# Powers of the state-space basis made on GpSimd during attention, and a channel loop fed by few large transfers

## The chip, the cores and the metric

The kernel runs on one core of a Trainium2 chip. The metric is the device time of one execution in microseconds. Some executions fall into a second, slower state of the chip.

## The reference

The reference computes a layer and all its gradients. `x` has 2048 tokens of 576 channels. Three parts are mixed by a gate:

```python
g = sigmoid((x * gate_w).sum(-1, keepdims=True))
a = attention(x, wqkv, wo)                 # 32 heads of 18 dimensions, softmax
# state-space convolution, per channel d with N = 128 complex modes:
logdA = exp(log_dt)[:, None] * (A_re + 1j * A_im)
K[d, l] = Re sum_n C[d, n] * exp(logdA[d, n] * l) * exp(log_dt[d]) * B[d, n]
b = causal_convolution(x, K) + x * Dskip   # the reference does it by FFT
out = g * a + (1 - g) * b
# ... and the vjp of out for x, wqkv, wo, the state-space parameters and gate_w
```

The kernel cuts the sequence of each channel into 16 pieces of 128 tokens. It therefore needs, for each channel and mode, the powers `exp(logdA * l)` for `l` from 0 to 127. This table, 576 x 128 x 128 complex numbers, is the **basis** of the title.

## The kernel before

The program has these stages: projections and the products of dO (here "first stage"), attention forward and backward, the weight gradients, and a loop over 18 blocks of 32 channels for the state-space part, followed by a final stage. In attention and in the channel loop the instructions of four engines stand in program order. SyncE, which issues nearly all transfers, is not among them; its queue is laid out by the scheduler:

```python
ctx.enter_context(tc.manual_schedule(engines={PE, Activation, DVE, Pool}))
```

In attention, each finished group of four score gradients `ds` is transposed by a transfer, and each finished gradient tile goes by a transpose, a pack on GpSimd, and a store:

```python
nc.vector.tensor_tensor(U["ds"][i][:, j, :], ps, U["PT"][i][:, j, :], op=A.mult)     # ds: 4 buffers
...
    nc.sync.dma_start_transpose(out=U["dsT", p][:, i % 2, :, :], in_=U["ds"][i]...)   # every 4th product

def store_grad(gb, g, which, t0):
    gT = work.tile([P, TPQ, 4, HP], BF, tag="gT", name="gT")
    nc.sync.dma_start_transpose(out=gT..., in_=gb)
    dtk = work.tile([P, TPQ, 4, DH], BF, tag="dtk", name="dtk")
    nc.gpsimd.tensor_copy(dtk, gT[:, :, :, 0:DH])
    nc.sync.dma_start(dqkv_d[...], dtk...)
```

In the channel loop, every block makes its own basis and its own shifted copies of `x` (cuts are marked):

```python
def m_load(b):                                    # eight shifted copies of x, 7 of them in a chain
    nc.sync.dma_start(xs[:, 0, :, :], xsub[:, :, d0:d0 + CB])
    nc.sync.dma_start(gyp[:, 0:SUB, :], gsub[:, :, d0:d0 + CB])
    for dl in range(1, NSUB):
        nc.sync.dma_start(xs[dl:P, dl, :, :], xs[0:P - dl, 0, :, :])
def m_mask(b):                                    # VectorE clears what was shifted in
    ...
    for dl in range(1, NSUB):
        nc.vector.tensor_scalar(xs[:, dl, :, :], xs[:, dl, :, :], msk[:, dl:dl + 1], None, op0=A.mult)
def kk(b, h, q):                                  # phase on TensorE, rounded on ScalarE
    ph = B_["ph"][(h, q)] = phase(b, h, q, 0)
    nc.scalar.activation(B_["kk"][h][:, 4 * q:4 * q + 4, :], ph, ACT.Identity, bias=magc, scale=1.0)
def ff(b, h, q):                                  # reduced on VectorE
    nc.vector.scalar_tensor_tensor(v_, v_, MAGIC, B_["ph"].pop((h, q)), op0=A.subtract, op1=A.subtract)
def sn(b, h): ...                                 # two sines and a square on ScalarE
def prod(b, h):                                   # products on VectorE, then a transpose by DMA
    nc.vector.tensor_tensor(E_[:, :, 1, :], B_["kk"].pop(h), B_["ab"][h], op=A.mult)
    nc.vector.scalar_tensor_tensor(E_[:, :, 0, :], B_["uk"].pop(h), 1.0, B_["ab"].pop(h), ...)
    nc.sync.dma_start_transpose(out=En..., in_=E_...)
```

Of the kernel before, what the change touches and what calls it, by code (L numbers as in the profile page):

```python
# [17 lines left out]
P = 128  # L18


def build(tc, aps, dbg_aps=None, stages=("s1", "attn", "post", "s4", "final")):
# [39 lines left out]
    with ExitStack() as gctx:  # L61
# [36 lines left out]
        spl_d = dram.tile([2, 3, D, N], BF, name="spl_d")  # L98
# [3 lines left out]
        omg_d = dram.tile([S], F32, name="omg_d")  # L102
        Md_d = dram.tile([D, SUB, MW], F32, name="Md_d")
        Kp_d = dram.tile([D, 2 * P], BF, name="Kp_d")
# [7 lines left out]
        with ExitStack() as ctx:  # L112
# [63 lines left out]
            for c in range(DC):  # L176
                nc.sync.dma_start_transpose(out=woT[:, :, c * P:(c + 1) * P], in_=wo_pad[:, c, :])
            cnt = 0
# [35 lines left out]
            for t in range(NT):  # L214
                if t % TB == 0:
                    tb = t // TB
                    go_b = work.tile([P, TB, D], BF, tag="go_b", name="go_b")
                    nc.sync.dma_start(go_b, go_v[:, t:t + TB, :])
                    d_a = d_a2[tb % 2]
                    for q in range(TB):  # L220
                        nc.vector.tensor_scalar(d_a[:, q, 0:D], go_b[:, q, :], g_t[:, t + q:t + q + 1], None, op0=A.mult)
                    d_aT = work.tile([P, TB, DC, P], BF, tag="d_aT", name="d_aT")
                    nc.sync.dma_start_transpose(out=d_aT.rearrange("p t c q -> p (t c) q"), in_=d_a.rearrange("p t d -> p (t d)"))
                psd = psB.tile([P, 2, 512], F32, tag="dO", bufs=1, name="ps_dO")
# [11 lines left out]
            with nc.allow_non_contiguous_dma(reason="gate values regrouped by 16 tokens"):  # L236
                nc.sync.dma_start(omg_d.rearrange("(t p) -> p t", p=P), omg_t)
# [11 lines left out]
            zero_bf = s1.tile([P, P], BF, name="zero_bf")  # L249
            nc.vector.memset(zero_bf, 0.0)  # L250
            for c, (d0, dsz) in enumerate(dch):
                nc.sync.dma_start(Kp_d[d0:d0 + dsz, 0:P], zero_bf[0:dsz, :])
# [5 lines left out]
            ltc = s1.tile([P, DC], BF, name="ltc")  # L258
            nc.gpsimd.memset(ltc, 0.0)
            for c, (d0, dsz) in enumerate(dch):  # L260
                nc.sync.dma_start(ltc[0:dsz, c:c + 1], log_dt.rearrange("(d o) -> d o", o=1)[d0:d0 + dsz, :])
            dtc = s1.tile([P, DC], F32, name="dtc")
            nc.scalar.activation(dtc, ltc, ACT.Exp)
            dtci = s1.tile([P, DC], F32, name="dtci")
            nc.scalar.mul(dtci, dtc, INV2PI)
            prm = []
            for r_, src_ap in enumerate((A_re, A_im, B_re, B_im, C_re, C_im)):
# [9 lines left out]
                if r_ < 2:  # L277
                    spl = s1.tile([P, 3, DC, N], BF, tag="spl", name="spl")
                    for c, (d0, dsz) in enumerate(dch):
                        sc_ = work.tile([P, N], F32, tag="adn", name="adn")  # L280
                        nc.vector.tensor_scalar(sc_[0:dsz, :], blk_[0:dsz, c, :], (dtc, dtci)[r_][0:dsz, c:c + 1], None, op0=A.mult)
                        for q in range(3):
                            nc.vector.tensor_copy(spl[0:dsz, q, c, :], sc_[0:dsz, :])
                            if q < 2:
                                nc.vector.tensor_tensor(sc_[0:dsz, :], sc_[0:dsz, :], spl[0:dsz, q, c, :], op=A.subtract)
                            nc.sync.dma_start(spl_d[r_, q, d0:d0 + dsz, :], spl[0:dsz, q, c, :])
# [20 lines left out]
            def zpow(p, nm):  # L307
# [7 lines left out]
                sh = newt("gk")  # L315
                nc.scalar.activation(sh, v_, ACT.Sin, scale=0.5 * TWO_PI * SIN_SAFE)
                nc.scalar.activation(v_, v_, ACT.Sin, scale=TWO_PI * SIN_SAFE)
# [25 lines left out]
        if "attn" in stages:  # L343
# [5 lines left out]
            with ExitStack() as ctx:  # L349
# [78 lines left out]
                def grad_tile(tag):  # L428
                    return work.tile([P, KB], BF, tag="gb" + tag, name="gb")

                def store_grad(gb, g, which, t0):
                    c0 = which * D + g * 4 * DH
                    gT = work.tile([P, TPQ, 4, HP], BF, tag="gT", name="gT")
                    nc.sync.dma_start_transpose(out=gT.rearrange("p t a b -> p t (a b)"), in_=gb)
                    dtk = work.tile([P, TPQ, 4, DH], BF, tag="dtk", name="dtk")
                    nc.gpsimd.tensor_copy(dtk, gT[:, :, :, 0:DH])
                    nc.sync.dma_start(dqkv_d[:, t0:t0 + TPQ, c0:c0 + 4 * DH], dtk.rearrange("p t a b -> p t (a b)"))
# [30 lines left out]
                def dv_burst(g, b, kq, half):  # L468
# [8 lines left out]
                    def ev():  # L477
# [6 lines left out]
                        if b == NQ - 1 and half == 1:  # L484
                            o_ = DKV[("v", g, kq)] = grad_tile("v")
# [3 lines left out]
                def dq_burst(g, b, p):  # L489
# [8 lines left out]
                    def ev():  # L498
# [5 lines left out]
                        if p == NST // 4 - 1:  # L504
                            o_ = U["dqa"] = grad_tile("q")
# [3 lines left out]
                def dk_half(g, b, p, h, st):  # L509
# [13 lines left out]
                    def ev():  # L523
# [3 lines left out]
                        if b == NQ - 1:  # L527
                            if p % 2 == 0:
                                DKV[("kb", g, kq)] = grad_tile("k")
                            o_ = DKV[("kb", g, kq)]  # L530
# [4 lines left out]
                    return ev  # L535

# [7 lines left out]
                for g0, nm, g, m in sorted(lds):  # L544
                    if g0 < 0:
                        load_piece(nm, g, m)
                    else:
                        at(("pre", g0), lambda nm=nm, g=g, m=m: load_piece(nm, g, m))
                NTOT = NU * NST
                for G in range(NTOT + OFF + 16):  # L550
# [113 lines left out]
                assert not todo, todo.keys()  # L664
# [102 lines left out]
        if "s4" in stages:  # L767
            CB = 32
            XB = 2 * CB
            GS = 16  # L770
            NBLK = D // CB
# [5 lines left out]
            dDs_d = dram.tile([1, D], F32, name="dDs_d")  # L777
# [3 lines left out]
            with ExitStack() as ctx:  # L781
# [3 lines left out]
                ident_f4 = pc.tile([P, P], F32, name="ident_f4")  # L785
                nc.vector.tensor_copy(ident_f4, ident_bf)
# [6 lines left out]
                magc = pc.tile([P, 1], F32, name="magc")  # L793
                nc.vector.memset(magc, MAGIC)
                lrow_i = pc.tile([64, P], mybir.dt.int32, name="lrow_i")
                nc.gpsimd.iota(lrow_i, pattern=[[1, P]], base=0, channel_multiplier=0)
                lrow = pc.tile([64, P], BF, name="lrow")
                nc.vector.tensor_copy(lrow, lrow_i)
                omp = pc.tile([P, SUB], F32, name="omp")
                nc.sync.dma_start(omp, omg_d.rearrange("(p t) -> p t", t=SUB))  # L800
                sidx_i = pc.tile([P, 1], mybir.dt.int32, name="sidx_i")
                nc.vector.tensor_scalar(sidx_i, pidx_i, NSUB - 1, None, op0=A.bitwise_and)
                scol = pc.tile([P, 1], F32, name="scol")
                nc.vector.tensor_copy(scol, sidx_i)
                msk = pc.tile([P, NSUB], F32, name="msk")
                for dl in range(NSUB):
                    nc.vector.tensor_scalar(msk[:, dl:dl + 1], scol, float(dl) - 0.5, None, op0=A.is_gt)
# [6 lines left out]
                xs = pc.tile([P, NSUB, SUB, CB], BF, name="xs")  # L814
                nc.vector.memset(xs[0:NSUB], 0.0)
                gyp = pc.tile([P, 2 * SUB, CB], BF, name="gyp")
                nc.vector.memset(gyp[:, SUB:2 * SUB, :], 0.0)
# [8 lines left out]
                xsub = x2.rearrange("(p t) d -> p t d", t=SUB)  # L826
                gsub = go2.rearrange("(p t) d -> p t d", t=SUB)
# [7 lines left out]
                def load_rx(xb):  # L835
# [3 lines left out]
                    gob = pw.tile([P, NB, XB], BF, tag="gob", name="gob")  # L839
                    nc.sync.dma_start(gob, go_v[:, :, d0:d0 + XB])  # L840
                    RXs[xb] = (RX, gob)

                def prep_rx(xb):
                    RX, gob = RXs[xb]
                    nc.vector.tensor_tensor(RX[:, CV0:CV0 + NB, :], gob[:, ::-1, :],
                                            omg_t[:, ::-1].unsqueeze(2).to_broadcast([P, NB, XB]), op=A.mult)
                    nc.vector.tensor_scalar(RX[:, CU1:CU1 + NS, :], RX[:, CU0:CU0 + NS, :], l1col, None, op0=A.mult)
                    nc.vector.tensor_scalar(RX[:, CV1:CV1 + NS, :], RX[:, CV0:CV0 + NS, :], l0col, None, op0=A.mult)

                def m_load(b):  # L850
                    d0 = b * CB
                    nc.sync.dma_start(xs[:, 0, :, :], xsub[:, :, d0:d0 + CB])
                    nc.sync.dma_start(gyp[:, 0:SUB, :], gsub[:, :, d0:d0 + CB])
                    for dl in range(1, NSUB):
                        nc.sync.dma_start(xs[dl:P, dl, :, :], xs[0:P - dl, 0, :, :])

                def m_mask(b):
                    nc.vector.tensor_tensor(gyp[:, 0:SUB, :], gyp[:, 0:SUB, :], omp.unsqueeze(2).to_broadcast([P, SUB, CB]), op=A.mult)
                    for dl in range(1, NSUB):
# [525 lines left out]
```

## Time and profile before

The time was 3787.35 us, the median of three runs (3780.48 to 3792.01). Cut by first and last instructions of each stage, the profiled execution of 3788.0 us splits so:

| stage | us |
|---|---|
| first stage, to the first exponential of attention | 256.0 |
| attention, to the last store of a gradient tile | 2140.3 |
| weight gradients | 227.2 |
| ramp, to the first scan of the channel loop | 95.2 |
| channel loop, first to last scan (17 blocks of 52.6) | 893.6 |
| last block and final stage | 175.7 |

The prediction below shows the slices, the table of busy time, the loop's groups and a list of waits, whose columns are who waited for whom, the total in us, how often, and the longest. Two more views of the kernel before stand behind the prediction. The first is the waits of the engines within attention; the columns are who waited for whom, the total in us, how often, and the longest:

```profile
ACT PT L646 <- PE ps_P L30: 41.6, 43, 4.3
...
DVE ds L655 <- DMA dsT<-ds: 7.5, 7, 2.3
```

ScalarE, the bound of attention, hardly waits, and VectorE practically never waits for a transpose to free a `ds` buffer. The second is the same list for the SyncE queue, in the same stretch:

```profile
SPq L661 <- DVE ds L655: 1072.9, 410, 6.5
...
SPq L437 <- POOL dtk L436: 54.6, 38, 3.8
```

SyncE spends half of attention waiting for the next `ds`, which means that it has nothing else to do and that the transposes leave at once. The second line is the one to remember: the gradient stores wait in this queue for GpSimd's pack, 54.6 us in all. GpSimd is idle then. Its packs in turn wait for the transposed tile (91 times, 931.2 us), so what holds such a store is the chain of transpose and pack ahead of it.

### The profile page before, as it was taken

What the parts mean: (1) busy time and instruction counts of PE and PEld (TensorE: products, weight loads), DVE (VectorE), ACT (ScalarE), POOL (GpSimd) and SP (SyncE); (2) the same over time, 40 slices, a digit from 0 to 9 for tenths busy, and PEclk for the clock granted to TensorE, in tenths of its full rate; (3) what the DMA queues carried; (4) which work ended last, traced back from release to release, by engine and by line L of the source; (5) the groups of instructions that cost most, each with busy time, mean ns of one, the idle gap of its engine ahead of it and who ended that gap; (6) DMA issues with size and microseconds to landing.
All of it is one profiled execution on the core that took longest, in us unless ns stands there. A gap on an engine that the chain in (4) does not pass through costs nothing. (4 is left out here: it accounts for less than half of the span.)

```text
span 3788.0 us, 67550 instructions
## 1 busy us (share of the span) xinstructions
PE 2907.0 (77%) x25832; PEld 1159.2 (31%) x25832; DVE 2891.6 (76%) x5099; ACT 2769.8 (73%) x5125; POOL 106.0 (3%) x210
## 2 busy tenths in 40 slices
PE   7969999999999999999999999487355444544421
PEld 2322323323323323333233232244133333333310
DVE  4616888878888888888888888253488888888867
ACT  4539999999999999999999997110466666666610
POOL 0000000000000000000000000100000000000000
PEclk9959999999999999999999999788565555555555
DMA  8536899898898998998888988945456556665456
GB/s 197 168 90 109 149 153 163 147 163 148 153 167 141 158 164 148 154 164 144 160 154 148 165 142 152 266 121 124 76 106 113 99 108 111 110 113 99 83 150 191
DMA packets 1869368, 537.02 MB, mean 142 GB/s; under 512 B 1778064, under 2 KB 1849818, under 8 KB 1869043
## 3 DMA queue, kind: packets, MB, share of 16 engines
q1 hardware_dynamic: 1869042, 532.70, 73.9%
q8 instruction: 202, 3.31, 0.4%
q14 instruction: 124, 1.01, 0.1%
HBM read 99.74 MB, written 60.96 MB: 42 GB/s over the span
## 5 line engine op out<-in xcount | busy, mean ns | idle before, releaser
L655 DVE TENSOR_TENSOR ds<-ps_P,PT 128x512 bf16<-128x512 f32 x2048 | 1332.5, 684 | 188.1 <-PE ps_P L30 159.5
L646 ACT ACTIVATE PT<-ps_P 128x512 bf16<-128x512 f32 x2048 | 1276.3, 628 | 54.6 <-PE ps_P L30 41.6
L650 ACT ACTIVATE eb<-ps_P 128x512 bf16<-128x512 f32 x2048 | 1291.8, 633 | 24.7 <-PE ps_P L30 24.6
L30 PE MATMUL ps_P<-dOaT,VaT_g 32*128 32x512 bf16 x2048 | 782.3, 387 | 13.8 <-DMA dOaT<-dOa 12.6
L30 PE MATMUL ps_P<-KaT_g,QaT_g 32*128 32x512 bf16 x2048 | 754.5, 381 | 37.9
L30 PE MATMUL ps_P<-QaT_g,KaT_g 32*128 32x512 bf16 x2048 | 639.3, 390 | 9.5 <-DMA QaT_g<-QaT_d 5.3
L30 PEld LDWEIGHTS <-VaT_g 32*128 32x128 bf16 x2048 | 179.9, 91 | 369.7 <-issue 354.9
L30 PEld LDWEIGHTS <-J_bf 128*128 128x128 bf16 x1876 | 162.0, 98 | 395.5 <-issue 289.6
L30 PE MATMUL accF<-ident_bf,J_bf 128*128 128x512 bf16 x1044 | 273.2, 385 | 0.0
L30 PEld LDWEIGHTS <-KaT_g 32*128 32x128 bf16 x2048 | 118.6, 92 | 393.6 <-issue 392.2
L30 PE MATMUL uvp<-RX,E1e 128*128 128x64 bf16 x1152 | 134.2, 290 | 107.5 <-DVE E1e L954 103.7
L30 PE MATMUL accO<-PT,Vtok_g 128*32 128x512 bf16 x2048 | 212.4, 399 | 0.1
L30 PE MATMUL tps<-RX,T0w 128*128 128x32 bf16 x576 | 38.4, 233 | 214.0 <-DVE yd L1089 190.5
L935 ACT ACTIVATE kk<-ph,magc 128x512 f32<-128x512 f32 x144 | 91.1, 686 | 147.6 <-DVE E1e L953 112.7
L30 PE MATMUL ph<-thr,lrow 3*128 3x512 bf16 x288 | 126.1, 567 | 88.0 <-ACT ab L928 60.5
L486 DVE TENSOR_TENSOR dvacc<-dvacc,accV 128x512 f32<-128x512 f32 x192 | 131.8, 686 | 75.5 <-PE accV L30 75.2
L30 PEld LDWEIGHTS <-QaT_g 32*128 32x128 bf16 x2048 | 156.9, 91 | 64.3 <-issue 46.5
L30 PE MATMUL accK<-dsT,Qtok_g 128*32 128x256 bf16 x4096 | 161.2, 278 | 4.7 <-DMA dsT<-ds 4.6
L30 PEld LDWEIGHTS <-E1e 128*128 128x128 bf16 x1152 | 125.3, 123 | 128.2 <-DVE E1e L954 127.7
L30 PE MATMUL accQ<-ds,Ktok_g 128*32 128x512 bf16 x2048 | 159.4, 389 | 0.0
L30 PE MATMUL accV<-eb,dOa 128*32 128x512 bf16 x2048 | 158.5, 386 | 0.0
L940 DVE SCALAR_TENSOR_TENSOR kk<-kk,ph 128x512 f32<-128x512 f32 x144 | 95.2, 683 | 72.6 <-ACT kk L935 72.6
(271 smaller groups left out, 3804.1 us busy)
## 6 DMA issues: line engine op xcount, KB each, us to landing
T0w<-Kp_d SPq DMA_DIRECT2D x36, 512.0 KB
dsT<-ds SPq DMA_TRANSPOSE x512
dqkv_d<-dtk SPq DMA_DIRECT2D x96, 72.0 KB
dqkv_tok<-dqkv_d SPq DMA_DIRECT2D x1, 6912.0 KB
Md_d<-mst SPq DMA_DIRECT2D x144, 36.0 KB
ga_d<-ga_st SPq DMA_DIRECT2D x16, 288.0 KB
dxm_d<-dxm SPq DMA_DIRECT2D x16, 288.0 KB
skw<-Md_d SPq DMA_DIRECT2D x72, 64.0 KB
```

The costliest lines, as they stand in the source:

```text
L30: return nc.tensor.matmul(out, lhsT=lhsT, rhs=rhs, start=start, stop=stop, **kw)
L486: nc.vector.tensor_tensor(o_, a_, acc, op=A.add)
L646: nc.scalar.activation(U["PT"][i][:, j, :], ps, ACT.Exp)
L650: nc.scalar.activation(e, ps, ACT.Exp)
L655: nc.vector.tensor_tensor(U["ds"][i][:, j, :], ps, U["PT"][i][:, j, :], op=A.mult)
L935: nc.scalar.activation(B_["kk"][h][:, 4 * q:4 * q + 4, :], ph, ACT.Identity, bias=magc, scale=1.0)
L940: nc.vector.scalar_tensor_tensor(v_, v_, MAGIC, B_["ph"].pop((h, q)), op0=A.subtract, op1=A.subtract)
```

## The change

The intent is to use the idle GpSimd. During attention it makes the whole basis by multiplying powers (16 powers of z, times 8 powers of z to the 16th), stores it from its own queue to DRAM, and the channel loop only loads it. The shifted and masked copies of `x` give way to layouts written to DRAM in the first stage, from which one large transfer per block reads. As GpSimd is now busy, the gradient pack was delayed by four steps of attention and its store by three more. The diff, cut to its core:

```diff
+ # first stage: zero fills and x, regrouped by channel block in 64-byte pieces
+ nc.sync.dma_start(Kp_d[:, 0:P, :]..., zero_bf...)
+ for r in range(NSUB - 1):
+     nc.sync.dma_start(xb_v[:, :, r, :]..., zero_bf...)
+ for k in range(NB):
+     nc.sync.dma_start(xb_v[:, k, NSUB - 1:XR, :]..., x_pad[:, k, 0:D]...)
  ... (gyb_d and gyr_d: the same for the scaled gradient, 16 + 4 stores)
  # attention
-     dtk = work.tile(...); nc.gpsimd.tensor_copy(dtk, gT[:, :, :, 0:DH])
-     nc.sync.dma_start(dqkv_d[...], dtk...)
+     def pack():
+         dtk = work.tile(...); nc.gpsimd.tensor_copy(dtk, gT[:, :, :, 0:DH])
+         return lambda: nc.sync.dma_start(dqkv_d[...], dtk...)
+     packs.append((now[0] + 4, pack))
+ def load_z(k):                                   # 36 of them, 2 buffers
+     ez[k] = work.tile([P, 2, CE], F32, tag="ez", bufs=2, name="ez")
+     nc.sync.dma_start(ez[k], par_d[:, 12:14, k * CE:(k + 1) * CE])
+ for k in range(D // CE):
+     eops.append((0.15, lambda k=k: nc.gpsimd.tensor_copy(T_[:, :, :, 1], ez.pop(k))))
+     ...  # small powers on GpSimd, load_z(k + 2), then per pair of channels 6 operations of 256 elements
+     nc.gpsimd.dma_start(E_d[:, q + 2 - EH:q + 2], Eo.pop(q // EH))        # 144 of them
+ if G % NST not in (1, 2) or G >= NTOT:
+     e_emit(G)                                    # some of these operations in each step of attention
  # channel loop
- m_mask, phase, ex, kk, ff, sn, prod
+ def load_e(b, h):
+     nc.sync.dma_start_transpose(out=E_..., in_=E_d[:, dG:dG + GS]...)
+ def load_en(b, h):
+     nc.sync.dma_start(En, E_d[:, dG:dG + GS])
+ def m_load(b):                                   # one transfer of 1 MB, one for gyp
+     nc.sync.dma_start(xs..., src)
+ # weights of the short convolution read with a stride: lhsT=T0w[:, :, h * GS + c_]
  ...
```

## The prediction

> **What bounds the kernel now.** I read the page's slices first, to find the stages, then one table of busy time per stage, then the VectorE groups and the waits of the last long stage.
>
> From the page of the kernel before, the busy tenths in 40 slices of 95 us:
>
> ```profile
> DVE  4616888878888888888888888253488888888867
> ACT  4539999999999999999999997110466666666610
> POOL 0000000000000000000000000100000000000000
> DMA  8536899898898998998888988945456556665456
> ```
>
> ScalarE is at 9 from slice 3 to slice 23 (attention), and never again. VectorE is at 8 from slice 28 to 37 (the channel loop). GpSimd does nothing worth a digit. So there are two long stages with different limits, and one idle engine. The table of busy time in stretches that I cut at the stage borders (projections, attention, weight gradients, ramp of the channel stage, channel loop, its last block, final) gives these two; the columns are the stretch and its length, then the busy us of PE, weight load, DVE, ACT, POOL, the granted clock, the DMA share and GB/s:
>
> ```profile
> 256.00:2398.00 2142.00, 2039.19 (x18320) 635.31 (x18319) 1757.14 (x2976) 2046.81 (x4096) 84.26 (x160) 0.98 0.87 151
> ...
> 2718.70:3612.30 893.60, 435.91 (x5094) 314.58 (x5094) 780.86 (x1383) 564.52 (x796) 0.00 (x0) 0.58 0.57 103
> ```
>
> Attention is ScalarE at 96%, with two kinds of 512-wide exponentials, 628 and 633 ns, and 66 us of waits for TensorE. GpSimd is busy 84 of 2142 us. The channel loop has 17 block starts in 893.6 us, 52.6 us each, and VectorE is busy 87% of it; TensorE has half its time free. The groups of VectorE in the steady part (us 2760 to 3600, 16 blocks; busy us and mean ns, then idle before):
>
> ```profile
> L985 DVE TENSOR_TENSOR tz<-HG,par 128x256 f32<-128x256 f32 x224 | 94.8, 423 | 5.5
> L940 DVE SCALAR_TENSOR_TENSOR kk<-kk,ph 128x512 f32<-128x512 f32 x128 | 84.7, 683 | 61.0 <-ACT kk L935 61.0
> L954 DVE SCALAR_TENSOR_TENSOR E1e<-uk,ab 128x2048 bf16<-128x2048 f32 x32 | 73.1, 2284 | 0.0
> L953 DVE TENSOR_TENSOR E1e<-kk,ab 128x2048 bf16<-128x2048 f32 x32 | 73.0, 2282 | 2.1 <-ACT kk L947 2.1
> ...
> L860 DVE TENSOR_SCALAR xs<-xs,msk 128x512 bf16<-128x512 bf16 x98 | 26.9, 346 | 0.0
> ...
> L858 DVE TENSOR_TENSOR gyp<-gyp,omp 128x512 bf16<-128x512 bf16 x14 | 9.6, 684 | 0.0
> L845 DVE TENSOR_TENSOR RX<-gob,omg_t 128x1024 bf16<-128x1024 bf16 x7 | 8.5, 1215 | 0.0
> ```
>
> Almost all of VectorE's waiting is before one group, the phase reduction, for ScalarE. The waits of the same stretch show that ScalarE in turn waits for VectorE's product; the two engines hand the making of the basis back and forth:
>
> ```profile
> ACT kk L935 <- DVE E1e L953: 107.8, 16, 6.7
> PE ybp L30 <- ACT ydi L1026: 88.1, 15, 6.0
> DVE kk L940 <- ACT kk L935: 61.0, 37, 2.8
> ```
>
> So the loop is bound by VectorE, and the basis is both its largest removable work and its only large wait.
>
> **What the skill says.** "GPSIMD Engine Reference", § 3.1 Elementwise: a two-input operation costs GpSimd about 2.6 cycles an element at 1.2 GHz, twice VectorE. The trace agrees: the product of 288 elements takes 691 ns, 2.4 ns an element with its fixed part. "SBUF — State Buffer", § Who interferes with whom: a VectorE instruction with two SBUF inputs blocks against a GpSimd instruction that reads SBUF, one with at most one SBUF input doesn't. VectorE's big groups in attention (ds 1332 us, and the accumulations) read one operand from PSUM, so by this page the new GpSimd work should not slow them; nothing in the trace of before tests it, since GpSimd is idle. "DMA: Bandwidth & Descriptors", § Specifications: below 512 B a transfer loses line rate, and an engine moves about 27 GiB/s. The packet records agree: medians 11 ns for 64 B, 13 for 128 B, 18 for 256 B, 159 for 4096 B (26 B/ns).
>
> **The change part by part.**
>
> *Channel loop, VectorE.* Removed per block: 8 phase reductions x 683 = 5.5 us, 2 x (2.28 + 2.28) = 9.1 us of products, 7 x 0.346 + 0.684 = 3.1 us of masks, and half of one RX preparation (1.22 + 0.46 + 0.46), 1.1 us: 18.8 us. What stays I add up from start to start in the timeline of one block: the scan 14 x 1.11 + 0.25 = 15.8, the weights wa, wb 4.1, Rw 2.1, yd 1.25, first pairs 1.85, second pairs 6.0: **31.1 us**. That is the new floor. ScalarE loses 4.8 (exp) + 5.5 (rounding) + 11.4 (sines, squares) + 2.6 (table loads) us and gains 1; it drops from 33 to about 10 us.
>
> *Channel loop, TensorE.* Loses 6.9 us of phases; about 19.5 us stay by the timeline. But the weights of the short convolution are now read with a stride of 64 B. The only strided weights of before (gyp, 32 columns) went at 74 ns each, 2.3 ns a column, where contiguous ones of 128 columns take 61 to 67 ns with their matmul. My estimate is 32 x 0.3 = 9.6 us a block instead of 2.1, so TensorE needs 27 us: below VectorE.
>
> *Channel loop, DMA.* Per block the new transfers, with median packet times over 16 engines: two basis transposes from DRAM (8192 x 18 ns: 9.2 us), the same basis untransposed (2 MB: 5.1), T0w in 8 KB rows (2.5, before 4.6), xs (2.5), gyp 0.4, Md twice as large (2.8), skw 0.9, par 1.25, RX and yd 3.3: **28 us**, and 31 with the packets' mean times under load. The scattered 64 B reads and seven shifted copies go. So DMA is nearly as long as VectorE. The queue of SyncE needs about 19 us a block (a 4096-wide transpose holds it 4.95 us), so it isn't the limit.
>
> I follow one block through: the loads run one or two blocks ahead; T0w of the block before lands some 9 us into the scan and has until 22 us; no VectorE instruction waits by more than 1 us. Allowing for DMA at 90% and more, I take **33 us a block**, against 52.6: 17 x 19.6 = 333 us gained.
>
> *Ramp.* From 2625 us to the first scan at 2719 it now takes 94 us: the shifted copies wait one on another, then phases, sines, products. After: one transpose, a 1 MB load, one short Toeplitz round trip through DRAM; about 40 us. Gain 54. Last block: 4.
>
> *Attention.* 288 pairs of channels x 6 operations of 256 elements. With 0.1 us fixed (a one-element GpSimd memset takes 0.10) and the rest of the 682 ns spread over 288 elements, 2.02 ns each, one takes 0.62 us: 1066 us. The powers: 36 x 28 small operations and copies, 7.1 us a group, 255 us. The 144 stores at about 1 us of descriptor writing: 144. In all 1465 beside the 84 there: 72% of 2142 us. It fits, and the code holds it back in the steps in which attention itself needs GpSimd. The stores move 37.7 MB in 2 KB packets, some 90 ns each: 107 us of the 16 engines, 5% on top of a share of 0.87. By median packet times the share is only two thirds, so the transposes of ds should still arrive. I allow **+10 us** for late products and gradient tiles.
>
> *First stage.* Two new layouts are stored in 64 B pieces: 2 x 16 x 2304 packets x 11 ns = 51 us of 16 engines, and fills and gyr 14 us, minus 3.5 us. SyncE's queue is in order and is occupied 104 of the first 128 us. The x pieces stand before the first projection's store, which has three buffers, so TensorE may stall behind them. I allow **+25 us**.
>
> Sum: 3787 - 333 - 54 - 4 + 10 + 25 = 3431, said as 3430.
>
> **The rivals.**
> 1. *DMA becomes the bound of the loop.* For it: 28 to 31 us of traffic against 31.1 of VectorE, and transposes of before already carry 22.7 ns instead of 18 under load. Against it: attention ran at a share of 0.87 with little waiting for data. It would give 36 to 38 us a block: 3480 to 3520.
> 2. *GpSimd stretches attention.* If its operations cost 40% more, or if it is blocked by VectorE, it needs over 2100 us, and the scaling of dO, the packing of gradients and the loads behind them in SyncE's queue slip. Against it: the PSUM operands. It would cost 50 to 150 us: 3470 to 3570.
> 3. *The first stage hides the new stores.* If the queue lets the projections' stores through, its cost is under 10 us, and with a loop at the floor of 31.1 us the time is about 3370.
> 4. *A chain through TensorE.* If strided weights take 0.4 us or more, T0w, short convolution, basis product and ybp in order take over 31 us. It would give some 35 us a block.
>
> **Range and chances.** The loop between 31.1 and 36 us gives -32 to +51; the first stage 5 to 45; attention 0 to 50. Not all at their end at once: 3360 to 3510, a little wider upwards as all surprises but one cost time. Slower than 3712 (no gain of 2%) needs attention to lose some 280 us: 5% with what I can't see.
>
> **What would show it.** In the trace after: starts of wa 31 to 34 us apart; VectorE over 90% busy in the loop; GpSimd 1400 to 1700 us busy, within attention; ScalarE still 95% there; the first attention exponential at 265 to 300 us instead of 256; the first scan some 40 us after the last weight gradient. I am wrong if VectorE in the loop waits for DMA, if the exponentials wait for GpSimd's tiles, or if GpSimd's operations take 0.8 us and more.

## The result, and the profile after

The kernel after is correct and took 3736.69 us, the median of four runs (3718.16 to 3738.7), beside 3789.68 us of the kernel before. The ratio is 0.985, with a 95% interval from 0.9818 to 0.9882. Here and below a ratio is the mean time of one kernel's fast runs over that of the other's fast runs of the same rounds, so it is not quite the ratio of the medians. The gain is 1.5%, where 9.4% had been predicted; 3736.69 lies outside the range of 3360 to 3510. The profiled execution, 3718.16 us, was the fastest of the four, some 18 us below the median, so the loss in the table below is a little smaller than that of a typical execution.

The stages show at once where it went (profiled executions, us):

| stage | before | after | change | predicted change |
|---|---|---|---|---|
| first stage | 256.0 | 293.2 | +37.2 | +25 |
| attention | 2140.3 | 2412.5 | **+272.2** | **+10** |
| weight gradients | 227.2 | 227.0 | -0.2 | 0 |
| ramp | 95.2 | 40.8 | -54.4 | -54 |
| channel loop | 893.6 | 571.5 | -322.1 | -333 |
| last block and final | 175.7 | 171.5 | -4.2 | -4 |
| total | 3788.0 | 3716.5 | -71.5 | -356 |

The page of the kernel after, busy tenths in 40 slices of 93 us, which answers to the slices in the prediction:

```profile
DVE  1643776867777677786678776878906188888877
ACT  1537888978899789897899887989601133333200
POOL 0007767766677667766776767674010000000000
DMA  9844788978978877986888877998994799999946
```

GpSimd now works at 6 to 7 tenths through attention, as intended. But ScalarE, at 9 in every slice of attention before, is at 7 to 9 now, and VectorE fell with it. In the last part DMA stands at 9 and ScalarE at 3. The same in numbers, from the table of busy time in stretches (length, then busy us of PE, weight load, DVE, ACT, POOL, granted clock, DMA share, GB/s) for attention and the channel loop:

```profile
293.20:2704.00 2410.80, 2108.47 (x18320) 631.93 (x18319) 1761.90 (x2976) 2058.17 (x4096) 1614.56 (x3111) 0.92 0.83 150
...
2973.50:3545.00 571.50, 318.50 (x4811) 297.18 (x4812) 501.85 (x1036) 186.88 (x387) 0.00 (x0) 0.68 0.99 235
```

In attention ScalarE does the same 2058 us of work as before (2047), but in 2411 us. It is busy 85% of the stretch, no longer 96%. So attention did not get more work on its bounding engine; that engine waits. The DMA share fell as well, from 0.87 to 0.83, which speaks against the transfers as what is short (e3 below settles it). In the loop VectorE is busy for 502 of 571.5 us, 88%, beside a DMA share of 0.99.

The costliest groups tell whether instructions became slower (busy us and mean ns, then idle before them):

```profile
L750 DVE TENSOR_TENSOR ds<-ps_P,PT 128x512 bf16<-128x512 f32 x2048 | 1327.0, 683 | 459.7 <-DMA dsT<-ds 221.0
...
L554 POOL TENSOR_TENSOR et<-eG,eT 128x256 f32<-128x256 f32 x1152 | 699.2, 628 | 36.8
...
L554 POOL TENSOR_TENSOR Eo<-et,et 128x256 bf16<-128x256 f32 x576 | 418.2, 726 | 43.5
```

They did not. VectorE's `ds` takes 683 ns beside a busy GpSimd, and took 684 ns beside an idle one. GpSimd's products take 628 ns, where 620 had been worked out. What is new is in the last column: `ds` waits 221 us for the transposes that free its buffers. The waits of the engines in attention show the chain that this starts:

```profile
ACT PT L741 <- PE ps_P L30: 303.1, 169, 15.4
DVE ds L750 <- DMA dsT<-ds: 221.0, 63, 17.4
...
PE ps_P L30 <- DVE ds L750: 77.4, 18, 15.4
```

Read it from the bottom of the chain: a transpose of `ds` comes late, VectorE cannot write the next `ds` (7.5 us of this wait before), TensorE gets no free tile for the next scores because `ds` has not emptied one, and ScalarE waits for TensorE (303.1 us, before 41.6). The rise of ScalarE's wait, 261 us, is nearly all that attention lost. So why do the transposes come late? The waits of SyncE's queue in the same stretch:

```profile
SPq L756 <- DVE ds L750: 830.0, 334, 4.9
SPq L561 <- POOL eT L608: 210.8, 27, 18.4
SPq L439 <- POOL dtk L438: 185.5, 40, 12.7
```

SyncE waits 210.8 us ahead of the loads of z (line 561), for GpSimd to have copied the z of an earlier group out of one of the two buffers, and 185.5 us ahead of the gradient stores (line 439), for GpSimd's pack. Before, the first kind did not exist and the second took 54.6. One such place in order of time; the columns are start, length, engine, line, operation and tiles:

```profile
566.69 1.21 SPq L434 DMA_TRANSPOSE gT<-gb  x1
575.84 0.37 SPq L439 DMA_DIRECT2D dqkv_d<-dtk  x1
576.30 1.88 SPq L756 DMA_TRANSPOSE dsT<-ds  x1
583.12 0.36 SPq L561 DMA_DIRECT2D ez<-par_d  x1
583.58 1.69 SPq L756 DMA_TRANSPOSE dsT<-ds  x1
```

Between 567.9 and 575.84 us, and again between 578.2 and 583.12, SyncE issues nothing at all. What it waits for stands in GpSimd's timeline:

```profile
575.39 0.42 POOL L438 COPY dtk<-gT 128x288 bf16<-128x288 bf16 x1
...
582.84 0.25 POOL L608 COPY eT<-ez 128x32 f32<-128x32 f32 x1
```

The pack ends at 575.8 and the store goes at 575.84; the copy of z ends at 583.1 and the next z is loaded at 583.12. Both are small instructions in the middle of basis products, and each lets a transpose of `ds` go that stood behind it. The delays also go round: over attention GpSimd's packs wait 175.9 us (47 times) for gradient tiles whose transposes stand in this same held queue. VectorE pays for the second one, as its timeline has it (in brackets, the idle time before and what ended it):

```profile
588.30 1.29 DVE L750 TENSOR_TENSOR ds<-ps_P,PT 128x512 bf16<-128x512 f32 x2 [4.76 <-DMA dsT<-ds]
```

How a load of z came to stand there is seen in the order of SyncE's queue as built; the numbers behind the names grow in program order:

```
242 gT_6594     <- gb_6512
243 dqkv_d_79   <- dtk_6790
244 dsT_6510    <- ds_6552
245 ez_7187     <- par_d_83
246 dsT_6670    <- ds_6625
```

The load `ez_7187` comes in the program long after `ds_6625`, some 14 steps of attention later, but its place in the queue is ahead. The scheduler, which lays out this queue, presumably took GpSimd to be ready earlier than it is; that reason is not shown, the order is. The same holds for the store: the program put it seven steps after its transpose, and here it follows directly. As the pack itself comes four steps later in GpSimd's program, a part of the store's wait is that written delay and not GpSimd's load; the two were not told apart.

Shown so far is that SyncE waits there and that `ds` waits for transposes. That one causes the other, and nothing else does, was left to the experiments.

### The profile page after: what moved, and what is told of

Same layout as the page of the kernel before. It is cut to its first block, busy times and chain, and to the rows that moved or that the text cites. A ratio compares the mean times of both kernels' runs of the same rounds, so it can differ in the third digit from the quotient of the medians.

```text
span 3716.5 us, 68768 instructions
## 1 busy us (share of the span) xinstructions
PE 2838.1 (76%) x25526; PEld 1134.1 (31%) x25526; DVE 2588.3 (70%) x4661; ACT 2381.6 (64%) x4691; POOL 1636.7 (44%) x3164
## 5 line engine op out<-in xcount | busy, mean ns | idle before, releaser
L750 DVE TENSOR_TENSOR ds<-ps_P,PT 128x512 bf16<-128x512 f32 x2048 | 1327.0, 683 | 459.7 <-DMA dsT<-ds 221.0
L741 ACT ACTIVATE PT<-ps_P 128x512 bf16<-128x512 f32 x2048 | 1273.1, 626 | 314.9 <-PE ps_P L30 303.1
L30 PE MATMUL ps_P<-dOaT,VaT_g 32*128 32x512 bf16 x2048 | 792.7, 401 | 128.6 <-DVE ds L750 77.4
L30 PE MATMUL ps_P<-KaT_g,QaT_g 32*128 32x512 bf16 x2048 | 737.0, 395 | 33.0
L554 POOL TENSOR_TENSOR et<-eG,eT 128x256 f32<-128x256 f32 x1152 | 699.2, 628 | 36.8
L30 PE MATMUL ps_P<-QaT_g,KaT_g 32*128 32x512 bf16 x2048 | 673.9, 403 | 10.3 <-issue 6.1
L554 POOL TENSOR_TENSOR Eo<-et,et 128x256 bf16<-128x256 f32 x576 | 418.2, 726 | 43.5
L30 PE MATMUL accF<-ident_bf,J_bf 128*128 128x512 bf16 x1044 | 291.4, 405 | 0.1
L30 PE MATMUL accK<-dsT,Qtok_g 128*32 128x256 bf16 x4096 | 170.2, 290 | 95.9 <-DMA dsT<-ds 95.7
L413 POOL TENSOR_TENSOR dOa<-dO_b,rl 128x288 bf16<-128x288 bf16 x32 | 21.5, 671 | 434.3 <-DVE rl L408 434.3
L30 PE MATMUL ps_proj<-xT,Wp 128*128 128x512 bf16 (+1 forms) x480 | 139.0, 397 | 43.6 <-ACT stg L208 40.1
L30 PEld LDWEIGHTS <-Qtok_g 128*32 128x32 bf16 x4096 | 91.1, 99 | 193.4 <-issue 135.1
## 6 DMA issues: line engine op xcount, KB each, us to landing
E_d<-Eo POOLq DMA_DIRECT2D x144, 256.0 KB, 3.2
```

The lines of the kernel that those rows point to most:

```text
L30: return nc.tensor.matmul(out, lhsT=lhsT, rhs=rhs, start=start, stop=stop, **kw)
L413: nc.gpsimd.tensor_tensor(da[:, :, :, 0:DH], U["dO"], rlb, op=A.mult)
L554: nc.gpsimd.tensor_tensor(out, a, b, op=op)
L741: nc.scalar.activation(U["PT"][i][:, j, :], ps, ACT.Exp)
```

## The experiments

Theory QUEUE: SyncE's queue issues in order, so the loads of z and the gradient stores, waiting for the busy GpSimd, hold up the transposes behind them. Rival TRAFFIC: the basis stores and the other added bytes take the DMA engines' time. Rival BLOCKED: GpSimd's work as such slows VectorE, or lets the gradients and dO slip. (The expectations of e1 to e5 call these rivals the DMA and the GPSIMD theory; in e9 to e12, QUEUE and TRAFFIC are about the first stage.) All twelve kernels below gave correct results. The stage columns in the table are of the profiled executions, and the loop's blocks are counted from the first to the last start of the weights `wa`; the kernel before ran beside each of them on the same chip (medians 3774.56 to 3789.89 us). Differences of some us between stages mean little: the kernel after and e1 to e5 share the code of the first stage and end it at 293.2 to 302.2 us, and e6, e7 and e9 to e12 share that of attention and take 2141.0 to 2155.4 us.

| kernel | median us | ratio to before | first stage | attention | loop per block |
|---|---|---|---|---|---|
| before | 3789.68 | 1 | 256.0 | 2140.3 | 52.35 |
| after | 3736.69 | 0.985 | 293.2 | 2412.5 | 33.40 |
| e1_z_pool | 3605.94 | 0.9526 | 302.2 | 2301.3 | 33.65 |
| e2_dtk_pool | 3702.96 | 0.9779 | 297.6 | 2381.6 | 33.35 |
| e3_both | 3473.48 | 0.9174 | 300.4 | 2155.4 | 33.56 |
| e4_sp_order | 3484.68 | 0.9194 | 300.5 | 2172.3 | 33.42 |
| e5_store_twice | 3494.36 | 0.9255 | 300.0 | 2193.3 | 33.44 |
| e6_spread | 3435.0 | 0.9094 | 284.0 | 2141.0 | 33.22 |
| e7_rx_first | 3427.58 | 0.9075 | 283.0 | 2145.4 | 32.72 |
| e8_before_sp_order | 3877.79 | 1.026 | 255.7 | 2240.5 | 52.34 |
| e9_par_early | 3451.69 | 0.9125 | 299.2 | 2151.7 | 32.78 |
| e10_par_pool | 3422.64 | 0.9042 | 276.3 | 2145.1 | 32.71 |
| e11_par_mid | 3441.5 | 0.9087 | 290.9 | 2149.6 | 32.78 |
| e12_par_mid_pool | 3435.2 | 0.9074 | 284.0 | 2155.4 | 32.55 |

A first form of the test, all of z loaded at once, never became a run: attention's pool of tiles would have needed 99.2 KB of a partition, and 95.1 KB were left. So the transfers were moved to another queue instead, where they wait behind the same GpSimd work but with no transposes after them.

**e1_z_pool: the loads of z on GpSimd's queue.**

```diff
-     nc.sync.dma_start(ez[k], par_d[:, 12:14, k * CE:(k + 1) * CE])
+     nc.gpsimd.dma_start(ez[k], par_d[:, 12:14, k * CE:(k + 1) * CE])
```

> The changed kernel with one edit: the 36 small loads of z (ez) go out on GpSimd's own DMA queue instead of SyncE's. Attention (first exponential to the gradient loads' end) took 2142 us before and 2411 us in the changed kernel, with 211 us of SyncE waiting before these loads for GpSimd. QUEUE theory (SyncE's in-order queue, in which the transposes of ds stand behind loads and stores that wait for GpSimd, makes the loss): attention shortens by 80 to 160 us, the total is 3580 to 3660 us, and the wait at ez disappears while that at the gradient stores (186 us) stays or grows. DMA theory (the 37.7 MB of basis stores make the transposes late): total within 15 us of the changed kernel's 3737. GPSIMD theory (GpSimd's work delays the scaled dO): 3730 to 3760, since 36 x 0.6 us are added to GpSimd.

**e2_dtk_pool: the 96 gradient stores on GpSimd's queue, right after the pack.**

```diff
-     return lambda: nc.sync.dma_start(dqkv_d[...], dtk...)
+     nc.gpsimd.dma_start(dqkv_d[...], dtk...)
+     return lambda: None
```

> The changed kernel with one edit: the 96 stores of packed gradients (dqkv_d from dtk) go out on GpSimd's own queue, right after the copy that packs them, instead of on SyncE's queue. SyncE waited 186 us before them in the changed kernel, 55 us in the kernel before. QUEUE theory: attention shortens by 50 to 140 us, total 3600 to 3690. DMA theory: 3725 to 3750. GPSIMD theory: 3740 to 3790, since 96 x 0.6 us are added to GpSimd.

**e3_both: both of these edits.**

> Both edits at once: SyncE's queue then waits for no GpSimd work at all but the scaled dO. QUEUE theory: attention falls to 2150 to 2230 us, total 3480 to 3560, and VectorE's wait for the transposes of ds (221 us) to under 30. DMA theory: attention stays above 2350 us. GPSIMD theory: attention stays above 2350 us or grows, with waits of the exponentials' matmuls for dOaT.

Attention took 111 us less in e1, 31 less in e2, and 257 less in e3. QUEUE's ranges held in e1 and, for attention, in e3, where the total came out 7 us below its range; e2 missed them, with 31 us instead of 50 to 140 and a total above 3690. The gains of e1 and e2 do not add up to that of e3, and the waits of SyncE's queue in attention say why. With the loads of z gone (e1), the stores wait longer than the 185.5 us of before:

```profile
SPq L439 <- POOL dtk L438: 239.2, 39, 13.0
```

With the stores gone (e2), the loads of z wait longer than 210.8 us:

```profile
SPq L562 <- POOL eT L609: 361.4, 30, 28.6
```

Each had been waiting partly in the shadow of the other: a queue that has just been held up by one arrives late at the next. With both gone (e3), no wait for a GpSimd product is left in the upper part of the list, and SyncE waits for `ds` as in the kernel before:

```profile
SPq L757 <- DVE ds L751: 1098.1, 391, 9.0
```

Among the waits of the engines in the same stretch of e3, ScalarE's is back near its old size of 41.6 us:

```profile
ACT PT L742 <- PE ps_P L30: 56.2, 56, 5.1
...
DVE ds L751 <- DMA dsT<-ds: 10.9, 6, 3.0
```

VectorE's wait for the transposes has fallen with it, from 221.0 us to 10.9.

All the bytes of the change, and all of GpSimd's products, are still there in e3, and attention is within 15 us of before, at a DMA share of 0.96. That refutes both rivals for all but those 15 us, which is about the size that the prediction had allowed for the whole stage.

**e4_sp_order: nothing moved, only SyncE's queue put into program order for attention.**

```diff
- manual_schedule(engines={PE, Activation, DVE, Pool})
+ manual_schedule(engines={PE, Activation, DVE, Pool, SP})
```

> The changed kernel with one word added: SyncE is put among the engines whose instructions keep the order of the program in attention, so the scheduler can't pull the z loads and gradient stores ahead of the transposes of ds (it pulled one z load some 14 attention steps ahead). All queues and transfers as in the changed kernel. QUEUE theory: the same gain as both edits, attention 2150 to 2240 us, total 3480 to 3570; the waits of SyncE at ez and dtk fall below 60 us together. DMA and GPSIMD theories: no gain, 3720 to 3750.

Attention took 2172.3 us, 240 less than in the kernel after, with the same transfers on the same queues. In the built queue `ez_7187` now stands behind the transpose of `ds_7129`, not ahead of that of `ds_6625`. So it is the order of the queue that costs, not the transfers and not the issuing engine.

**e5_store_twice: e3 with every basis store done a second time, into a DRAM tile that nobody reads.**

```diff
      nc.gpsimd.dma_start(E_d[...], Eo...)
+     nc.gpsimd.dma_start(E2_d[...], Eo...)
```

> The kernel of the third run (both edits: z loads and gradient stores on GpSimd's queue; 3473 us, attention 2155 us) in which every basis store is issued a second time, to a DRAM tensor that nobody reads: 37.7 MB more of the same traffic and 144 more descriptor writings on GpSimd. QUEUE theory: the traffic is affordable, attention grows by 0 to 40 us, total 3475 to 3520. DMA theory (the stores, at a DMA share of 0.9 and more, are what delays the transposes): attention grows by 100 to 250 us, total over 3570.

Another 37.7 MB of stores, with 144 more instructions on GpSimd to issue them, cost attention 38 us. That is at the upper end of what QUEUE allowed. So the stores may not be free, but a single set of them does not explain 272 us.

**e8_before_sp_order: the control, the edit of e4 in the kernel before.**

> Control: the kernel before, with SyncE's instructions kept in program order in attention (the one word of the fourth run). QUEUE theory: before the change nothing important in SyncE's queue waited for GpSimd (55 us before gradient stores), so the word brings nothing: attention 2125 to 2160 us, total within 25 us of before. Rival: program order on SyncE is better by itself, whatever GpSimd does; then this kernel is more than 60 us faster than before.

This missed both expectations: attention became 100 us *longer*, and the kernel 2.6% slower. The waits of its SyncE queue, to hold against the 54.6 us of before:

```profile
SPq L437 <- POOL dtk L436: 180.1, 86, 4.3
```

The kernel before has its store right behind transpose and pack in the program. In program order SyncE then waits for each pack, with the transposes of `ds` behind it; the scheduler had moved those stores to a later place. So program order is not better in itself. In the changed kernel it is, because there the program holds the stores and the loads of z back itself. But most of this loss did not come by the transposes of `ds`: VectorE's wait for them rose only from 7.5 to 26.4 us. Its wait for GpSimd's `prod` rose from 13.1 us to:

```profile
DVE dl L421 <- POOL prod L415: 81.2, 8, 13.1
```

GpSimd's timeline shows why, for the last of these waits (9.71 us, to 2209.26):

```profile
2207.39 0.43 POOL L436 COPY dtk<-gT 128x288 bf16<-128x288 bf16 x1 [6.42 <-DMA gT<-gb]
...
2208.53 0.69 POOL L415 TENSOR_TENSOR prod<-dOa,Ob 128x288 f32<-128x288 bf16 x1
```

The product stood behind a pack, and the pack waited for a transposed tile that SyncE had issued only at 2204.74, after the store of the tile before. So here the lateness passes from one queue in order to another. That is the mechanism of QUEUE on another path, with no basis work and no new transfers; no run took the parts of this loss apart.

**e6_spread: e3 with the fills and the 16 stores of `x` taken from in front of the projections and handed out two and one per group.** In the kernel after, they hold SyncE's queue before the first store of a projection. The timeline of SyncE in e3, where this part is as in the kernel after:

```profile
37.88 16.20 SPq L188 DMA_DIRECT2D xb_d<-zero_bf  x7
54.12 30.84 SPq L190 DMA_DIRECT2D xb_d<-x_pad  x16
85.06 1.61 SPq L225 DMA_DIRECT2D KaT_d<-stg  x1
```

In the kernel before that first store goes at 37.20 us; here at 85.06. The three buffers of the projections are full by then, and ScalarE waits; from the waits of the engines in e3's first 300 us:

```profile
ACT stg L208 <- DMA KaT_d<-stg: 41.8, 1, 41.8
```

```diff
- (1 fill of Kp_d, 7 fills and 16 stores of xb_d ahead of the projections)
  for g in range(NG):
      ... projections of group g, with their stores
+     for k in (2 * g, 2 * g + 1):
+         nc.sync.dma_start(xb_v[:, k, NSUB - 1:XR, :]..., x_pad[:, k, 0:D]...)
+     (and one fill)
```

> The kernel of the third run, with the x pieces and zero fills (24 transfers that hold SyncE's queue from 37 to 85 us, ahead of the first projection's store) moved in program order: three of them after each of the 8 groups of projections. My theory for the first stage (300 us against 256 before): the in-order queue again, TensorE stands 38 us because the three projection buffers can't be stored. Then the first stage ends at 258 to 275 us and the total is 3430 to 3450. Rival: the engines' time for 64-byte packets sets the stage, whatever the order; then it ends at 290 us or later and the total stays within 10 us of 3473.

The wait is gone and the total came out as expected (3435.0), but the stage ends at 284.0 us. That is 16 less than in e3 and short of the 258 to 275 that were expected; it is also below the rival's 290. That the total fits is in part luck: of the 40 us between the two profiled executions 14 came in attention and 6 in the loop, where the edit changes nothing. So the order explains some 16 of the 44 us by which e3's first stage exceeds that before. In what remains, the wait ahead of attention's first product stands out: TensorE stands idle 22.3 us there in e6, against 5.3 in the kernel before, and SyncE works off some 50 us of small transfers for the state-space parameters in front of attention's first load. In the kernel before these ran beside the projections. Four more runs went after that tail.

**e7_rx_first: e6, with one load of the channel loop issued earlier within its block.** ScalarE waited for it 82.0 us in 500 us of the loop in e6, by the waits of that stretch:

```profile
ACT RX L926 <- DMA RX<-xr_d: 82.0, 7, 13.4
```

```diff
+ if sb is not None and sb % 2 == 0:
+     load_rx(sb // 2)
  load_par(i + 1); load_en(i + 1, 0); load_en(i + 1, 1); m_load(mb)
- if sb is not None and sb % 2 == 0:
-     load_rx(sb // 2)
```

A third buffer for this tile, the plainer way, did not fit (the loop's pool of tiles would have needed 181 KB, and 174.2 KB were left).

> The sixth kernel, with the loads of RX in the channel loop moved ahead of the loads of par, E1n and xs of the same iteration. In the loop every second block takes 31.2 us, the VectorE floor of the prediction, and the others 34 to 40 us; in those ScalarE waits some 12 us for RX and TensorE for ScalarE. Theory: the late RX makes the difference; blocks then take 31.2 to 33 us throughout and the total falls by 20 to 40 us below the sixth kernel's. Rival: DMA at a share of 1.0 sets the pace of a pair of blocks; then something else is late instead, 33.4 us a block on average stays, and the total is within 10 us of the sixth kernel's.

The loop fell by 8 us, not by 20 to 40. The wait vanished from the top of the list, and another took its place in the same view of e7; it had been 59.2 us in e6:

```profile
PE psM L30 <- DMA gyp<-gyb_d: 127.2, 16, 11.5
```

The DMA share of this loop is 1.03. Moving one transfer ahead put another behind, which fits the rival's view that the transfers set the pace.

**e9 to e12: the parameter tail of the first stage.** All four start from e7. e9 places the parameter work ahead of the products of dO, e11 places it after the second group of projections, e10 only moves its 30 loads to GpSimd's queue, and e12 does e11 and e10 together.

```diff
  # e10, e12
-     nc.sync.dma_start(blk_[0:dsz, c, :], src_ap[d0:d0 + dsz, :])
+     nc.gpsimd.dma_start(blk_[0:dsz, c, :], src_ap[d0:d0 + dsz, :])
  # e9, e11: the block "dt_b ... spar(11, nwi)" moved up, unchanged
```

> e7 with the parameter work (transposes, products and stores of the state-space parameters) placed ahead of the dO products in the program, so that its transfers stand in SyncE's queue among the projections' stores, as they stand in the kernel before, and no longer in one tail of some 50 us between the last reversed x and the first load of attention. QUEUE (what is left of the first stage's growth is that tail: TensorE idle 22.3 us ahead of attention's first product in e6, against 5.3 in the kernel before): the first attention exponential moves from 283 us to 260-268, the idle stretch falls below 8 us, time 15-23 us less than e7, about 0.902 of the kernel before. TRAFFIC (the 64-byte stores take the DMA engines' time, wherever they stand): first exponential at 278 or later, time within 5 us of e7 (0.9075 of the kernel before).

> e7 with only the 30 loads of the parameter blocks moved from SyncE's queue to GpSimd's, which is idle then. QUEUE: these 30 loads hold SyncE's queue about 0.49 us each in e6, 15 us of the tail of 50, so the first attention exponential moves from 283 us to 264-272, time 10-18 us less than e7. TRAFFIC: no change beyond 5 us. If the tail is held by the chain of the parameter products on VectorE and not by the number of transfers in the queue, also no change.

> e7 with the whole parameter work placed after the second group of projections, where the kernel before has it in effect (its transfers left there between 66 and 159 us), so that it runs beside projections that TensorE bounds and stands ahead neither of dO's transposes (as in e9) nor of attention's loads (as in e7). QUEUE (a tail of parameter transfers costs what TensorE waits behind it, wherever TensorE has nothing else): first attention exponential 258-272 instead of 283, TensorE's idle stretch ahead of attention under 8 us, time 10-25 us below e7 (ratio 0.901 to 0.905). TRAFFIC (the new 64-byte stores stretch the stage by themselves): first exponential 278 or later, time within 5 us of e7.

> e11 with the 30 parameter loads on GpSimd's queue as well. QUEUE: beside the projections SyncE has room, so this gives at most 5 us on e11. If e11 leaves the projections' stores waiting behind loads that have not landed, this removes it and is 5 to 15 us faster than e11.

e9 missed QUEUE's expectation, and TRAFFIC's in time (its ratio is 0.9125): the stage ends at 299.2 us. The idle stretch ahead of attention is gone, but TensorE now waits elsewhere, for the transposed gradient that the products of dO need and that stands behind the parameter transfers in the queue. From its waits in the first 290 us:

```profile
PE ps_dO L30 <- DMA d_aT<-d_a: 42.2, 3, 27.1
```

e11 got rid of most of both waits (the stretch ahead of attention is 5.9 us, as QUEUE said) and still ends at 290.9 us: the products of dO, which ran partly beside the projections in e6, now come after them, at a granted clock of 0.50 and a DMA share of 0.90 between 190 and 240 us. Its first stage is where TRAFFIC put it, and by the ratios its time is too: 0.9087 beside 0.9075 of e7 is some 5 us. e12 ends the stage 7 us before e11; its stretch ahead of attention is 5.5 us. e10 ends it 6.7 us before e7, less than the 11 to 19 expected; by the ratios it is 12 us faster, as QUEUE said, but the intervals overlap. Both gains in the stage are within the 9 us by which the first stage differs between kernels with the same code there, so neither is shown. In this stage no single place of the tail is the cause. At least 20 us of its growth stay open; the queue's order, the extra 64-byte stores and the falling clock were not told apart.

The fastest kernel of all is **e10_par_pool** with 3422.64 us, a ratio of 0.9042 (0.9015 to 0.9068); e7, on another chip, has 0.9075 (0.906 to 0.9089), and the two intervals overlap. Both beat the kernel before and the kernel after.

## Why the prediction was right or wrong

**The bound of the loop and its floor: right in the sum.** The loop takes 33.4 us a block, where 33 had been said. Every second block or so starts 31.2 us after the one before it, which is the floor of VectorE's work that was added up (31.1), and the others take 32 to 41, one at the start 30.2. VectorE's share is 88%, not over 90%: in those others it waits ahead of `yd` (36.6 us over the loop) for TensorE's short convolution, and that for the load of its weights `T0w` (60.8 us). So "no VectorE instruction waits by more than 1 us" was wrong. DMA was put at 28 to 31 us a block; a share of 0.99 of 33.6 us is 33. The transfers were mis-sized, and it was the 2 us allowed above the floor that made the number come out. Rival 1, DMA as the bound at 36 to 38 us, was thus half right: the DMA engines are full, but at 33.4 us.

**Strided weights: mis-sized, and harmless.** The 32 products with weights at a stride of 64 B were put at 9.6 us a block. They take 2.62 us in the trace (82 ns each, with their weight loads). "TensorE: Matmul & The Clock Gate", § Weight-path perf modes, says of the fast weight load that it reads "packed or strided" columns; the trace fits that, since the contiguous weights of the kernel before took 67 ns, and reading it would have spared the estimate. Rival 4 had no ground.

**Ramp and last block: right,** 54.4 us for 54, and 4.2 for 4.

**GpSimd's durations and the absence of blocking: right.** 628 ns for 620, a total of 1637 us for "1400 to 1700", and `ds` at 683 ns. That the total is so near is partly luck: the 144 stores, put at about 1 us each without a measurement, took 0.58, and the powers took 336 us in place of 255. The step from the operands in PSUM to "should not slow them" held. This refutes the mechanism of rival 2, dear or blocked operations, though the rival had the sign of the loss and its stage.

**The first stage: within its range, too low.** 37 us for 25. The reason that was given, the `x` pieces ahead of the first projection's store, is real and worth some 16 us (e6). The rest is open.

**Attention: the step that failed** is "I allow **+10 us** for late products and gradient tiles." It measured +272 us, and that is all of the miss: with +10 in its place, the changes of the other stages give 3454 us, within the range. The step asked whether GpSimd's work fits into attention's time, and whether the transfers fit into the DMA engines' share. Both do: with nothing changed but the queues (e3), the stage takes 15 us more than before, at a DMA share of 0.96. It did not ask what else waits where the busy engine's products are awaited. The prediction saw that the queue of SyncE is in order and used it for the first stage; it named "the loads behind them in SyncE's queue" in rival 2, but only in case GpSimd's operations were dear. It relied on "the code holds it back in the steps in which attention itself needs GpSimd", which is the program's order, while SyncE's queue has an order of its own. The 54.6 us that SyncE waited for `dtk` before the change were on view in the kernel before. They were the sign that a store behind a GpSimd product holds this queue even while GpSimd is idle. The prediction did name what came, "Slower than 3712 (no gain of 2%) needs attention to lose some 280 us", and gave it 5% "with what I can't see"; what it left out was the built order of this queue.

What would have made the prediction wrong was listed as "if the exponentials wait for GpSimd's tiles". They do not wait for them directly. They wait for TensorE, that for VectorE, that for a transpose, and the transpose for its turn. So that sign, looked for by itself, would not have shown the error; "ScalarE still 95% there" did, with 85%.

## What to carry to other kernels

When work is given to an idle engine, list every transfer that waits for that engine, find the queue in which it waits, and look at what stands behind it: in this kernel the queue, which is in order, turned the lateness of unimportant transfers into that of all that followed. Attention lost 272 us, and 257 of them came back once these transfers stood elsewhere (e3). Here such transfers did best in the queue of the engine that they wait for, or far enough back; and where a scheduler lays out the queue, read the order it built, since the delays written in the program do not bind it. When two such waits are found, test them together, since each hides the other.

## What the Trainium skill lacked or had wrong

- "DMA: Bandwidth & Descriptors", § Issuing engines are not separate DMA queues, says that issuing from several engines only saves the time to start a transfer, usually small. It does not say what a waiting transfer does to those behind it in the same issuing queue. Moving 132 small transfers from SyncE to GpSimd, with the same bytes, took the time from 3736.69 to 3473.48 us; the waits concerned were 210.8 and 185.5 us, and reordering the queue alone (e4) gained nearly as much.
- "GPSIMD Engine Reference", § 3.1 Elementwise, gives about 2.6 cycles an element at 1.2 GHz (2.2 ns) and no figure for what an instruction costs besides. Here sums and differences of 16, 64 and 128 elements took 226, 319 and 454 ns: 2.1 ns an element, worked out from the last two, as the page has it, and some 0.2 us fixed. Up to 64 elements, the fixed part is the larger one. Products with one operand broadcast took 439 and 658 ns for 128 and 256 elements, which is 1.7 ns an element and less than the page's figure.
- No page has a time for weights read with a stride. The runs show 82 ns for a pair of load and product (128 columns at 64 B, 32 moving columns).
